# A block-attention and feed-forward kernel: token chunks of 512 against chunks of 512, 384 and 512

## The chip, the core and the metric

The kernel runs on one core of a Trainium2 chip. The metric is the device time of one execution in microseconds (us). Three runs of the kernel before took 1269.4, 1270.7 and 1272.47 us; the median is 1270.7 us.

## The reference: what is computed

Two stages follow each other. The first is attention over 8 batches, 8 heads, 576 positions and a head size of 64, masked by blocks of 64 positions. The second is a feed-forward network over the 4608 tokens that the attention gives.

```python
# _attn_ref: q, k, v of 8 x 8 x 576 x 64
scores = scale * np.matmul(q, k.transpose(0, 1, 3, 2))
mask = block_i >= block_j                      # blocks of 64
scores = np.where(mask, scores, -1000000000.0)
scores = scores - np.max(scores, axis=-1, keepdims=True)
attn = np.exp(scores)
attn = attn / (np.sum(attn, axis=-1, keepdims=True) + 1e-09)
return np.matmul(attn, v)
# _moe_ref: x of 4608 x 512, w_in 512 x 2048, w_out 2048 x 512
h = x @ w_in
g = np.where(h >= 1, h, np.where(h <= -1, 0.0, (h + 1) ** 2 / 4))
return g @ w_out
```

## The kernel before

**Attention.** Heads are worked on in pairs, four pairs a batch, 32 pairs in all. `attention_steps` is a generator that gives one step at a time, eight steps a pair, 258 in all. Within a step TensorE makes scores (`product`, two matmuls a tile, L482 and L485), transposes of the softmax that an earlier step left (`transposed`, L552), products of the softmax with v (`weighted`, L591) and transposes of q and k (L401, L442). VectorE (DVE) and ScalarE (ACT) do the softmax: maximum (L505), exponential (L509), sum, reciprocal, scaling (L515). Each of these TensorE results lies in a PSUM bank that `work_bank` hands out, and the bank is free for its next user once DVE and ACT have read it. `store_x` (or `both`, for the first two batches) writes the result, split into a high and a low half, into the rings `xh` and `xl`, which hold 1536 tokens.

**Feed-forward.** The tokens go in nine chunks of 512 (`TCH`), and each chunk over 16 slices of the hidden size. One slice has two half-steps. `ffn_in` makes 12 matmuls of 512 columns into the one bank of `ph` (4 parts of 128 of the model size, times 3 products of high and low halves; L770), and then ACT, DVE and POOL make `gh` and `gl` of it (L779, L780, L783, L784, L785). `ffn_out` makes 12 matmuls of 512 columns (L794 and L799: four token tiles of 128, times 3 products) into four banks `po`, which hold the sums of the chunk over all 16 slices. `ffn_out` of a slice comes one half-step after `ffn_in` of the next one. Each slice loads 512 KB of `w_out` (`wo`, L787) from DRAM; two buffers hold them.

**PSUM.** The eight banks are: three `ps_w` for the attention, one `ps_h` for `ph`, four `ps_o` for the sums. Before the feed-forward starts, the attention takes banks of `ps_o` and `ps_w` by turns; after that it has the three of `ps_w`.

**Order.** The loop at the end of the kernel runs the attention's steps. From step `START` = 36 on it runs one feed-forward half-step after each attention step; what is left after step 257 runs by itself. There are 288 half-steps: 222 beside the attention and 66 after it. A scheduler then moves single instructions where data or banks come late; from about 300 us on, the order on TensorE is that of the code but for a few rows. Names: `qk` is the transposed input of q and k, `prr` a softmax tile after its way through a DMA copy, `x` (`x32`) the attention's output before it is split.

Of the kernel before, what the change touches and what calls it, by code (L numbers as in the profile page):

```python
# [8 lines left out]
F32 = mybir.dt.float32  # L9
F32R = mybir.dt.float32r  # L10
# [13 lines left out]
def block_attn_then_ffn(  # L24
# [9 lines left out]
    nc = tc.nc  # L34
    B, H, S, D = q.shape
    NT, DM = out.shape
    DF = w_in.shape[1]
    P = 128
# [4 lines left out]
    NPAIR = H // 2  # L43
    NCC = DM // P
    NFC = DF // P
    TCH = 512
    NCH = NT // TCH
    NTT = TCH // P
    RING = 3 * TCH
    G0 = 256  # L50
    G1 = S - G0
# [14 lines left out]
    att1 = ctx.enter_context(tc.tile_pool(name="att1", bufs=1))  # L66
# [3 lines left out]
    ffn = ctx.enter_context(tc.tile_pool(name="ffn", bufs=2))  # L70
# [2 lines left out]
    dram = ctx.enter_context(tc.tile_pool(name="dram", bufs=1, space=bass.MemoryType.DRAM))  # L73
    ps_w = ctx.enter_context(tc.tile_pool(name="ps_w", bufs=3, space=bass.MemoryType.PSUM))
    ps_h = ctx.enter_context(tc.tile_pool(name="ps_h", bufs=1, space=bass.MemoryType.PSUM))
    ps_o = ctx.enter_context(tc.tile_pool(name="ps_o", bufs=NTT, space=bass.MemoryType.PSUM))

    banks = {"free": True, "n": 0}

    def work_bank(name):  # L80

        banks["n"] += 1
        if banks["free"] and banks["n"] % 2:
            return ps_o.tile([P, 512], F32, tag="po", name=name)
        return ps_w.tile([P, 512], F32, tag="work", name=name)


# [140 lines left out]
    spare = {"n": 0, "of": []}  # L228

    def as_float32r(src, plain):  # L230

        if plain:
            if not spare["of"]:
                spare["of"] = [t_[:, :NTL, :, :].rearrange("p t h d -> p (t h d)") for t_ in vsr]
                spare["of"].append(att1.tile([P, S], F32R, tag="x32", name="prs")[:, :TCH])
# [3 lines left out]
            if src.shape[1] > TCH:  # L239
                moved.append(spare["end"])  # L240
            for i, dst in enumerate(moved):
                n = min(TCH, src.shape[1] - i * TCH)
                nc.sync.dma_start(dst[:, :n].bitcast(F32), src[:, i * TCH : i * TCH + n])
            return moved
        moved = []
        for c0 in range(0, src.shape[1], TCH):
            n = min(TCH, src.shape[1] - c0)
            pool, tag = ((conv, "bits"), (conv2, "work"))[c0 > 0]
            dst = pool.tile([P, TCH], F32R, tag=tag, name="prr")
            nc.sync.dma_start(dst[:, :n].bitcast(F32), src[:, c0 : c0 + n])  # L250
            moved.append(dst)
        return moved


    class Pair:
# [141 lines left out]
        def turned_raw(self, j):  # L397

            ps = work_bank("ps_qk")
            for t in range(NTL):  # L400
                nc.tensor.transpose(  # L401
                    ps[:, t * P : (t + 1) * P].bitcast(F32R), self.qk[:, j * NTL + t, :, :], ident_r
                )
            self.parted(
                lambda x: x[:, j, :SM].rearrange("p (c t) -> p c t", t=NTL),
                ps[:, :SM].rearrange("p (t c) -> p c t", t=NTL),
            )
            for a, bt, hi0 in ((qa, qb, 0), (ka, kb, D)):
# [138 lines left out]
                nc.vector.tensor_tensor(out=lo, in0=ps, in1=hi.bitcast(F32), op=ALU.subtract)  # L547

        def transposed(self, out, parts, c0, n):
            src = parts[c0 // TCH][:, c0 % TCH : c0 % TCH + n] if self.hop else parts[0][:, c0 : c0 + n]  # L550
# [210 lines left out]


    def ffn_in(c, fc):
        at = (c * TCH) % RING
        ph = ps_h.tile([P, 512], F32, tag="ph", name="ph")
        fs = slice(fc * P, (fc + 1) * P)
        xs = slice(at, at + TCH)
        for cc in range(NCC):
            for i, (w, x) in enumerate(((wih, xh), (wih, xl), (wil, xh))):
                nc.tensor.matmul(  # L770
                    ph, w[:, cc, fs], x[:, cc, xs],
                    start=(cc == 0 and i == 0), stop=(cc == NCC - 1 and i == 2),
                )


        t_ = ffn.tile([P, TCH], F32, tag="t", name="t")
        gh = ffn.tile([P, TCH], F32R, tag="gh", name="gh")
        gl = ffn.tile([P, TCH], F32R, tag="gl", name="gl")
# [5 lines left out]
        nc.scalar.copy(gh, t_)  # L784
        nc.gpsimd.tensor_tensor(out=gl, in0=t_, in1=gh.bitcast(F32), op=ALU.subtract)  # L785
        wo = ffn.tile([P, 2, DM], F32R, tag="wo", name="wo")
        nc.sync.dma_start(wo.bitcast(F32), wo_split[fc])  # L787
        return gh, gl, wo

    def ffn_out(po, c, fc, gh, gl, wo):  # L790
        for tt in range(NTT):
            ts_ = slice(tt * P, (tt + 1) * P)
            for w in range(2):
                nc.tensor.matmul(  # L794
                    po[tt], gh[:, ts_], wo[:, w, :], start=(fc == 0 and w == 0), stop=False
                )
        for tt in range(NTT):
# [4 lines left out]
        for tt in range(NTT):  # L802
# [7 lines left out]
            r0 = c * TCH + tt * P  # L810
            nc.sync.dma_start(out[r0 : r0 + P, :], ob)

    def feed_forward():
        prev = None
        for c in range(NCH):
            for fc in range(NFC):
                cur = (c, fc, *ffn_in(c, fc))
                yield
                if prev is not None:
                    if prev[1] == 0:  # L820
                        po = [ps_o.tile([P, DM], F32, tag="po", name="po") for _ in range(NTT)]
                    ffn_out(po, *prev)
                    yield
                prev = cur
        ffn_out(po, *prev)
        yield
# [10 lines left out]
    converted = 0  # L837
    for i, _ in enumerate(attention_steps()):
        if i < START:
            want = (i + 1) * EARLY // START  # L840
        else:
            want = max(
                EARLY + (i - START + 1) * (NFC // GROUP * PART - EARLY) // (2 * NFC - 4 * GROUP),
                ((i - START) // (2 * GROUP) + 1) * PART,
            )
# [39 lines left out]
```

## Time and profile before

| what | value |
|---|---|
| median of three runs | 1270.7 us (1269.4 to 1272.47) |
| profiled execution, its own time | 1269.69 us |
| its span, first to last instruction | 1267.9 us |
| TensorE matmul busy | 1200.1 us, 95% |
| VectorE busy | 887.0 us, 70% |
| ScalarE busy | 703.2 us, 55% |
| GpSimd busy | 394.6 us, 31% |
| mean granted TensorE clock | 0.981 |

The busy time of TensorE counts a matmul from its start to the modelled end of its way through the array, so that neighbours overlap: what a matmul costs is the distance from its start to the next one's start. The share over the whole span mixes four stages: the attention alone (to about 155 us), the attention of the first batches beside the first chunk (to about 286 us), the attention beside the other chunks (to about 1080 us), and the last chunks alone.

### The profile page before, as it was taken

How to read it: one execution, taken by the hardware profiler on the slowest of the kernel's cores; microseconds unless marked ns; L12 is line 12 of the kernel's file. 1: busy time of each engine (PE TensorE's matmuls, PEld its weight loads, DVE VectorE, ACT ScalarE, POOL GpSimd, SP SyncE). 2: the span in 40 equal slices, each digit the busy share in tenths (PEclk: the TensorE clock that was granted, in tenths of full speed). 3: DMA queues.
4: the chain of work that ended last, by engine and by line, in shares of the span. 5: the costliest groups of instructions: out<-in, count | busy, mean ns of one | idle time of the engine just before them, and what ended most of it. 6: DMA issues, size and time to landing. Idle time of an engine off the chain costs nothing.

```text
span 1267.9 us, 20253 instructions
## 1 busy us (share of the span) xinstructions
PE 1200.1 (95%) x6280; PEld 998.8 (79%) x6280; DVE 887.0 (70%) x2188; ACT 703.2 (55%) x1827; POOL 394.6 (31%) x430
## 2 busy tenths in 40 slices
PE   5888889899999999999999999999999999999998
PEld 4666667678888888888888888888888888888886
DVE  8898877758777777777777777787777777322222
ACT  5787656646566655665656655566556555222222
POOL 3555655522222222222222222222222222222222
PEclk9888988999999999999999999999999999999999
DMA  5566666667888655555554655465556433422432
GB/s 158 167 176 215 203 228 197 217 198 237 260 273 266 215 162 158 154 175 163 156 162 145 187 157 152 138 189 153 160 154 190 137 128 118 132 87 98 133 100 100
DMA packets 185259, 215.43 MB, mean 170 GB/s; under 512 B 113840, under 2 KB 132272, under 8 KB 184384
## 3 DMA queue, kind: packets, MB, share of 16 engines
q1 hardware_dynamic: 185152, 214.14, 54.9%
q8 instruction: 50, 0.82, 0.3%
q14 instruction: 57, 0.47, 0.1%
HBM read 134.74 MB, written 31.98 MB: 131 GB/s over the span
## 4 chain that ended last, share of the span: by engine, by line
PE 69%; DVE 16%; ACT 6%; issue 5%; DMA 1%; POOL 1%; SPq 1%; ACTq 0%; POOLq 0%; DVEq 0%
PE ph L770 29%; PE po L794 15%; PE po L799 7%; PE ps_av L591 7%; PE ps_s L482 4%; ACT pr L509 3%; PE ps_s L485 3%; DVE t L780 2%; PE ps_t L552 2%; DVE t L783 2%; ACT t L779 2%; DVE pb L547 2%; DVE nm L505 2%; DVE sm L491 1%; DVE pr L515 1%
## 5 line engine op out<-in xcount | busy, mean ns | idle before, releaser
L785 POOL TENSOR_TENSOR gl<-t,gh 128x512 fp32r<-128x512 f32 x144 | 187.5, 1302 | 510.2 <-ACT gh L784 333.2
L794 PE MATMUL po<-wo,gh 128*128 128x512 f32 x1152 | 296.1, 397 | 0.5 <-DMA wo<-wo_split 0.3
L794 PEld LDWEIGHTS po<-wo,gh 128*128 128x128 f32 x1152 | 212.5, 189 | 44.5 <-DMA wo<-wo_split 0.7
L770 PE MATMUL ph<-xh,wih 128*128 128x512 f32 x576 | 232.9, 404 | 1.6 <-DVE t L783 1.6
L770 PE MATMUL ph<-xh,wil 128*128 128x512 f32 x576 | 228.8, 397 | 0.0
L770 PE MATMUL ph<-xl,wih 128*128 128x512 f32 x576 | 227.8, 396 | 0.5 <-DVE xl L627 0.5
L780 DVE SCALAR_TENSOR_TENSOR t<-t 128x512 f32<-128x512 f32 x144 | 101.5, 705 | 168.0 <-ACT t L779 165.2
L779 ACT ACTIVATE t<-ph 128x512 f32<-128x512 f32 x144 | 85.9, 597 | 173.8 <-PE ph L770 173.8
L509 ACT ACTIVATE pr<-ps_s,nm 128x128 f32<-128x128 f32 (+3 forms) x256 | 134.1, 527 | 60.5 <-DVE nm L505 58.4
L784 ACT CAST gh<-t 128x512 fp32r<-128x512 f32 x144 | 89.5, 621 | 120.3 <-DVE t L783 120.0
L799 PE MATMUL po<-wo,gl 128*128 128x512 f32 x576 | 155.6, 392 | 0.0
L482 PE MATMUL ps_s<-ka,qa 68*128 68x288 f32 (+4 forms) x384 | 135.3, 367 | 15.0 <-ACT pr L509 5.4
L379 POOL TENSOR_TENSOR vsr<-vn,vsr 128x256 fp32r<-128x256 f32 (+1 forms) x96 | 55.2, 576 | 246.2 <-ACT vsr L378 244.6
L770 PEld LDWEIGHTS ph<-xh,wil 128*128 128x128 f32 x576 | 109.5, 190 | 23.8
L770 PEld LDWEIGHTS ph<-xh,wih 128*128 128x128 f32 x576 | 109.8, 191 | 21.7 <-DVE t L783 2.3
L799 PEld LDWEIGHTS po<-wo,gl 128*128 128x128 f32 x576 | 108.7, 189 | 23.1
L505 DVE TENSOR_REDUCE nm<-ps_s 128x1 f32<-128x128 f32 (+3 forms) x256 | 118.8, 482 | 10.4 <-PE ps_s L485 9.4
L770 PEld LDWEIGHTS ph<-xl,wih 128*128 128x128 f32 x576 | 109.7, 190 | 20.5 <-DVE xl L627 0.9
L485 PE MATMUL ps_s<-kb,qb 128*128 128x288 f32 (+4 forms) x384 | 121.1, 322 | 0.0
L515 DVE TENSOR_SCALAR pr<-pr,sm 128x128 f32<-128x128 f32 (+3 forms) x256 | 107.3, 440 | 5.4
L783 DVE TENSOR_TENSOR t<-ph,t 128x512 f32<-128x512 f32 x144 | 98.7, 686 | 2.2
L491 DVE TENSOR_SCALAR sm<-sm 128x1 f32<-128x1 f32 (+1 forms) x224 | 52.0, 232 | 68.3 <-ACT pr L509 65.7
(111 smaller groups left out, 1871.4 us busy)
## 6 DMA issues: line engine op xcount, KB each, us to landing
wo<-wo_split SPq DMA_DIRECT2D x144, 512.0 KB, 3.5
prr<-pr SPq DMA_DIRECT2D x96, 192.0 KB, 2.5
prr<-pr SPq DMA_DIRECT2D x72, 256.0 KB, 2.8
out_dram<-ob SPq DMA_DIRECT2D x36, 256.0 KB, 2.9
bits<-in_moe_w_in_dram SPq DMA_DIRECT2D x32, 256.0 KB, 3.5
bits<-in_moe_w_out_dram SPq DMA_DIRECT2D x32, 256.0 KB, 3.0
wo_split<-ws SPq DMA_DIRECT2D x16, 512.0 KB, 2.9
qa<-qb SPq DMA_DIRECT2D x63, 128.0 KB, 2.4
```

Of the source, the lines that this page charges most:

```text
L482: nc.tensor.matmul(ps, qa[:KA, j, c0 : c0 + P], ka[:KA, j, k0 : k0 + n], start=first, stop=False)
L485: nc.tensor.matmul(ps, qb[:, j, c0 : c0 + P], kb[:, j, k0 : k0 + n], start=False, stop=last)
L505: nc.vector.tensor_reduce(out=nm[:, i : i + 1], in_=ps[:, cs], axis=AX.X, op=ALU.max, negate=True)
L509: nc.scalar.activation(pr[:, cs], ps[:, cs], AF.Exp, bias=nm[:, i : i + 1], scale=1.0, accum_out=sm[:, i : i + 1],)
L515: nc.vector.tensor_scalar_mul(pr[:, cs], pr[:, cs], sm[:, i : i + 1])
L770: nc.tensor.matmul(ph, w[:, cc, fs], x[:, cc, xs], start=(cc == 0 and i == 0), stop=(cc == NCC - 1 and i == 2),)
L779: nc.scalar.activation(t_, ph, AF.Relu, bias=0.5, scale=0.5)
L780: nc.vector.scalar_tensor_tensor(out=t_, in0=t_, scalar=1.0, in1=t_, op0=ALU.min, op1=ALU.mult)
L783: nc.vector.tensor_tensor(out=t_, in0=ph, in1=t_, op=ALU.max)
L785: nc.gpsimd.tensor_tensor(out=gl, in0=t_, in1=gh.bitcast(F32), op=ALU.subtract)
L794: nc.tensor.matmul(po[tt], gh[:, ts_], wo[:, w, :], start=(fc == 0 and w == 0), stop=False)
L799: nc.tensor.matmul(po[tt], gl[:, ts_], wo[:, 0, :], start=False, stop=fc == NFC - 1)
```

## The change

The chunks of tokens become: one of 512, eight of 384, two of 512, eleven in all. A chunk of 384 has three token tiles, so its sums need three banks. `ps_o` has three banks now, and the eighth bank (`ps_x`) serves the sums of the 512 chunks and, while chunks of 384 run, the attention: there it takes turns "wwwx", four banks in all. Before the feed-forward starts the turns are "woxwowo", seven banks.

The chunks of 384 do not divide the ring of 1536 tokens at the offset of 512: the chunks that start at tokens 1280 and 2816 lie over its end, at places 1280 to 1535 and 0 to 127. Each of their matmuls in `ffn_in` becomes two, of 256 and of 128 columns, with the same weights.

The pace is given by a table. `BEGIN` is the attention step at which each chunk starts: 36, 68, 99, 119, 139, 163, 183, 203, 227; the last two chunks would start at 259 and 279, past the attention's end at 257. The 32 half-steps of a chunk are spread over the steps to the next entry: 31 to 32 steps (chunks 0, 1 and 8), 20 steps (2, 3, 5, 6) or 24 (4, 7). Of 352 half-steps, 287 are run by step 257 and 65 after it.

```diff
+    NARROW = 384
+    CHUNKS = [(0, TCH)] + [(TCH + i * NARROW, NARROW) for i in range(MID)]
+    CHUNKS += [(t0, TCH) for t0 in range(CHUNKS[-1][0] + NARROW, NT, TCH)]
+    NTT = NARROW // P
...
+    ps_x = ctx.enter_context(tc.tile_pool(name="ps_x", bufs=1, space=bass.MemoryType.PSUM))
     ps_o = ctx.enter_context(tc.tile_pool(name="ps_o", bufs=NTT, space=bass.MemoryType.PSUM))
-    banks = {"free": True, "n": 0}
+    banks = {"turns": "woxwowo", "n": 0}
     def work_bank(name):
+        turns = banks["turns"]
+        turn = turns[banks["n"] % len(turns)]
         banks["n"] += 1
-        if banks["free"] and banks["n"] % 2:
+        if turn == "o":
             return ps_o.tile([P, 512], F32, tag="po", name=name)
+        if turn == "x":
+            return ps_x.tile([P, 512], F32, tag="px", name=name)
         return ps_w.tile([P, 512], F32, tag="work", name=name)
...
     def ffn_in(c, fc):
-        at = (c * TCH) % RING
+        t0, n = CHUNKS[c]
+        at = t0 % RING
+        runs = [(0, at, min(n, RING - at))]
+        if at + n > RING:
+            runs.append((RING - at, 0, at + n - RING))
         for cc in range(NCC):
             for i, (w, x) in enumerate(((wih, xh), (wih, xl), (wil, xh))):
-                nc.tensor.matmul(
-                    ph, w[:, cc, fs], x[:, cc, xs],
-                    start=(cc == 0 and i == 0), stop=(cc == NCC - 1 and i == 2),
-                )
+                for c0, x0, m in runs:
+                    nc.tensor.matmul(
+                        ph[:, c0 : c0 + m], w[:, cc, fs], x[:, cc, x0 : x0 + m],
+                        start=(cc == 0 and i == 0 and c0 == 0),
+                        stop=(cc == NCC - 1 and i == 2 and c0 + m == n),
+                    )
...
     def ffn_out(po, c, fc, gh, gl, wo):
-        for tt in range(NTT):
+        for tt in range(CHUNKS[c][1] // P):
...
                         po = [ps_o.tile([P, DM], F32, tag="po", name="po") for _ in range(NTT)]
+                        if CHUNKS[prev[0]][1] > NARROW:
+                            po.append(ps_x.tile([P, DM], F32, tag="px", name="po"))
...
+    BEGIN = [START]
+    for t0, n in CHUNKS[1:]:
+        ready = -(-(t0 + n) // S) * 8 * NPAIR + 3
+        BEGIN.append(max(ready, BEGIN[-1] + 20))
+    BEGIN[1] = START + 2 * NFC
...
+            c = sum(i >= x for x in BEGIN) - 1
+            left = BEGIN[c + 1] - BEGIN[c] if c + 1 < len(BEGIN) else 2 * NFC
+            due = 2 * NFC * c + min(2 * NFC, (i - BEGIN[c] + 1) * 2 * NFC // left)
...
-            banks["free"] = False
-            next(ffn_steps, None)
+            banks["turns"] = "www" if i < BEGIN[1] + 2 else "wwwx"
+            for _ in range(due - done):
+                next(ffn_steps, None)
+            done = due
```

The first place is on TensorE, in the second step of a pair of heads: the last transposes of q and k (`turned_last`, L442 before, L452 now), with the transposes and scores ahead of it and the feed-forward half-step behind it. The brackets name whose progress a row waits for. Before:

```order
L799 MATMUL po<-wo,gl 128x512 x3
L552 MATMUL ps_t<-ident_r,prr 128x128 [waits DMAHW0_49,DVE_49]
L552 MATMUL ps_t<-ident_r,prr 128x128 x3
L482 MATMUL ps_s<-ka,qa 128x384 [waits Activation_49]
L485 MATMUL ps_s<-kb,qb 128x384
L442 MATMUL ps_qk<-ident_r,qk 128x128 [waits DVE_49,PE_49]
L770 MATMUL ph<-xh,wih 128x512
```

Now, beside a chunk that has 20 steps:

```order
L785 MATMUL ph<-xh,wil 128x384
L562 MATMUL ps_t<-ident_r,prr 128x128 [waits DMAHW3_49,PE_49]
L562 MATMUL ps_t<-ident_r,prr 128x128 x3
L492 MATMUL ps_s<-ka,qa 128x384 [waits PE_49]
L495 MATMUL ps_s<-kb,qb 128x384
L452 MATMUL ps_qk<-ident_r,qk 128x128 [waits Activation_49]
L810 MATMUL po<-wo,gh 128x512 [waits DMAHW5_49]
```

The transpose waited for DVE, which read the bank of three users before; now it waits for ACT, which reads the bank of four users before, and the half-step behind it is another one.

The second place is on TensorE too, in the chunk that starts at token 1280: the matmuls of `ffn_in`. Before, and below it now:

```order
L770 MATMUL ph<-xh,wih 128x512
L770 MATMUL ph<-xl,wih 128x512
L770 MATMUL ph<-xh,wil 128x512
L770 MATMUL ph<-xh,wih 128x512
L770 MATMUL ph<-xl,wih 128x512
```

```order
L815 MATMUL po<-wo,gl 128x512 x2
L785 MATMUL ph<-xh,wih 128x256 [waits DVE_49]
L785 MATMUL ph<-xh,wih 128x128
L785 MATMUL ph<-xl,wih 128x256
L785 MATMUL ph<-xl,wih 128x128
L785 MATMUL ph<-xh,wil 128x256
L785 MATMUL ph<-xh,wil 128x128
```

Each matmul of 384 columns stands there as one of 256 and one of 128, each with a weight load of its own, 24 in the half-step in place of 12; in the other narrow chunks it is one row of 128x384.

More of the change, by code (lines that the diff above doesn't have):

```diff
@@ L46, in block_attn_then_ffn @@
     TCH = 512
-    NCH = NT // TCH
-    NTT = TCH // P
+    NARROW = 384
+    BANK = 512
+    MID = (NT - 3 * TCH) // NARROW
+    CHUNKS = [(0, TCH)] + [(TCH + i * NARROW, NARROW) for i in range(MID)]
+    CHUNKS += [(t0, TCH) for t0 in range(CHUNKS[-1][0] + NARROW, NT, TCH)]
+    NTT = NARROW // P
     RING = 3 * TCH
@@ L234, in as_float32r @@
                 spare["of"] = [t_[:, :NTL, :, :].rearrange("p t h d -> p (t h d)") for t_ in vsr]
-                spare["of"].append(att1.tile([P, S], F32R, tag="x32", name="prs")[:, :TCH])
+                spare["of"].append(att1.tile([P, S], F32R, tag="x32", name="prs")[:, :BANK])
                 spare["end"] = att1.tile([P, G0 + P], F32R, tag="pa11", name="pre")[:, :BLK]
@@ L238, in as_float32r @@
             spare["n"] += 1
-            if src.shape[1] > TCH:
+            if src.shape[1] > BANK:
                 moved.append(spare["end"])
             for i, dst in enumerate(moved):
-                n = min(TCH, src.shape[1] - i * TCH)
-                nc.sync.dma_start(dst[:, :n].bitcast(F32), src[:, i * TCH : i * TCH + n])
+                n = min(BANK, src.shape[1] - i * BANK)
+                nc.sync.dma_start(dst[:, :n].bitcast(F32), src[:, i * BANK : i * BANK + n])
             return moved
         moved = []
-        for c0 in range(0, src.shape[1], TCH):
-            n = min(TCH, src.shape[1] - c0)
+        for c0 in range(0, src.shape[1], BANK):
+            n = min(BANK, src.shape[1] - c0)
             pool, tag = ((conv, "bits"), (conv2, "work"))[c0 > 0]
-            dst = pool.tile([P, TCH], F32R, tag=tag, name="prr")
+            dst = pool.tile([P, BANK], F32R, tag=tag, name="prr")
             nc.sync.dma_start(dst[:, :n].bitcast(F32), src[:, c0 : c0 + n])
@@ L549, in transposed @@
         def transposed(self, out, parts, c0, n):
-            src = parts[c0 // TCH][:, c0 % TCH : c0 % TCH + n] if self.hop else parts[0][:, c0 : c0 + n]
+            src = parts[c0 // BANK][:, c0 % BANK : c0 % BANK + n] if self.hop else parts[0][:, c0 : c0 + n]
             if self.hop:
@@ L763, in ffn_in @@
     def ffn_in(c, fc):
-        at = (c * TCH) % RING
-        ph = ps_h.tile([P, 512], F32, tag="ph", name="ph")
+        t0, n = CHUNKS[c]
+        at = t0 % RING
+        ph = ps_h.tile([P, TCH], F32, tag="ph", name="ph")[:, :n]
         fs = slice(fc * P, (fc + 1) * P)
-        xs = slice(at, at + TCH)
+        runs = [(0, at, min(n, RING - at))]
+        if at + n > RING:
+            runs.append((RING - at, 0, at + n - RING))
         for cc in range(NCC):
             for i, (w, x) in enumerate(((wih, xh), (wih, xl), (wil, xh))):
-                nc.tensor.matmul(
-                    ph, w[:, cc, fs], x[:, cc, xs],
-                    start=(cc == 0 and i == 0), stop=(cc == NCC - 1 and i == 2),
-                )
-        t_ = ffn.tile([P, TCH], F32, tag="t", name="t")
-        gh = ffn.tile([P, TCH], F32R, tag="gh", name="gh")
-        gl = ffn.tile([P, TCH], F32R, tag="gl", name="gl")
+                for c0, x0, m in runs:
[4 more added lines that the diff above has]
+                    )
+        t_ = ffn.tile([P, TCH], F32, tag="t", name="t")[:, :n]
+        gh = ffn.tile([P, TCH], F32R, tag="gh", name="gh")[:, :n]
+        gl = ffn.tile([P, TCH], F32R, tag="gl", name="gl")[:, :n]
         nc.scalar.activation(t_, ph, AF.Relu, bias=0.5, scale=0.5)
@@ L796, in ffn_out @@
                 )
-        for tt in range(NTT):
+        for tt in range(CHUNKS[c][1] // P):
             ts_ = slice(tt * P, (tt + 1) * P)
@@ L801, in ffn_out @@
             return
-        for tt in range(NTT):
+        for tt in range(CHUNKS[c][1] // P):
             ob = conv.tile([P, DM], F32, tag="bits", name="ob") if tt % 2 else conv2.tile(
@@ L809, in ffn_out @@
                 nc.vector.tensor_copy(ob, po[tt])
-            r0 = c * TCH + tt * P
+            r0 = CHUNKS[c][0] + tt * P
             nc.sync.dma_start(out[r0 : r0 + P, :], ob)
@@ L814, in feed_forward @@
         prev = None
-        for c in range(NCH):
+        for c in range(len(CHUNKS)):
             for fc in range(NFC):
@@ L836, in block_attn_then_ffn @@
     ffn_steps = feed_forward()
-    converted = 0
+    BEGIN = [START]
[3 more added lines that the diff above has]
+    BEGIN[1] = START + 2 * NFC
+    converted = done = 0
     for i, _ in enumerate(attention_steps()):
@@ L841, in block_attn_then_ffn @@
         else:
+            c = sum(i >= x for x in BEGIN) - 1
+            left = BEGIN[c + 1] - BEGIN[c] if c + 1 < len(BEGIN) else 2 * NFC
+            due = 2 * NFC * c + min(2 * NFC, (i - BEGIN[c] + 1) * 2 * NFC // left)
             want = max(
-                EARLY + (i - START + 1) * (NFC // GROUP * PART - EARLY) // (2 * NFC - 4 * GROUP),
-                ((i - START) // (2 * GROUP) + 1) * PART,
+                EARLY + due * (NFC // GROUP * PART - EARLY) // (2 * NFC - 4 * GROUP),
+                ((due - 1) // (2 * GROUP) + 1) * PART,
             )
```

## The prediction

> **What bounds the kernel.** I read the page's engine table and slices first, then busy time by stage, then single matmuls.
>
> ```profile
> PE 1200.1 (95%) x6280; PEld 998.8 (79%) x6280; DVE 887.0 (70%) x2188; ACT 703.2 (55%) x1827; POOL 394.6 (31%) x430
> PE   5888889899999999999999999999999999999998
> DVE  8898877758777777777777777787777777322222
> PEclk9888988999999999999999999999999999999999
> ```
>
> ```profile
> 0.00:155.00 155.00, 121.89 (x629) 98.26 (x630) 134.84 (x394) 109.91 (x326) 78.98 (x103) 0.93 0.61 185
> 155.00:286.00 131.00, 115.49 (x523) 88.82 (x522) 91.54 (x224) 74.29 (x207) 61.20 (x74) 0.91 0.66 208
> 286.00:1080.00 794.00, 779.88 (x4327) 661.13 (x4326) 610.76 (x1500) 474.71 (x1223) 210.46 (x219) 1.00 0.58 175
> 1080.00:1268.00 188.00, 182.79 (x807) 150.64 (x805) 49.89 (x73) 44.27 (x74) 43.99 (x34) 0.99 0.33 108
> ```
>
> The columns are the stretch, its length, then busy us of PE, PEld, DVE, ACT and POOL, the granted clock, the DMA share and GB/s. Three limits show. To 155 us DVE is busy 134.84 of 155 (87%) and PE waits for it. From 286 to 1080 us PE is busy 779.88 of 794: 14.1 us of idle time in the whole stage in which the change acts. After 1080 us PE runs alone. So in the stage that matters a matmul added is time added, and a wait removed can give back only what PE loses now.
>
> How fast PE can go is in the starts of its matmuls and weight loads:
>
> ```profile
> 704.87 0.39 PE L770 MATMUL ph<-xh,wil 128*128 128x512 f32 x1
> ...
> 706.91 0.39 PE L770 MATMUL ph<-xh,wil 128*128 128x512 f32 x1
> ```
>
> ```profile
> 702.62 1.31 PE L591 MATMUL ps_av<-pb,vsr 128*128 128x320 f32 x8
> 703.77 0.33 PE L591 MATMUL ps_av<-pcs,vsr 128*128 128x64 f32 x2
> ...
> 707.88 1.03 PE L591 MATMUL ps_av<-pa,vsr 128*128 128x256 f32 x8
> 708.75 2.03 PE L794 MATMUL po<-wo,gh 128*128 128x512 f32 x8
> ```
>
> ```profile
> 707.77 1.00 PEld L591 LDWEIGHTS ps_av<-pa,vsr 128*128 128x128 f32 x8
> 708.69 0.77 PEld L794 LDWEIGHTS po<-wo,gh 128*128 128x128 f32 x4
> ```
>
> Between the first two rows lie nine distances: (706.91 - 704.87)/9 = 0.227 us for 512 columns. The group at 707.88 has, by the code, four matmuls of 256 and four of 128 columns in pairs, a mean of 192; they take (708.75 - 707.88)/8 = 0.109 us each, and their weight loads (708.69 - 707.77)/8 = 0.115 us each. By columns, 192 would take 0.085 us. So short matmuls go at the pace of their weight loads, 0.109 to 0.115 us.
>
> **The waits that a fourth bank can touch.**
>
> ```profile
> PE ps_qk L442 <- DVE x L614: 8.9, 23, 0.4
> PE ps_s L482 <- ACT pr L509: 5.2, 17, 0.3
> ```
>
> ```profile
> 711.30 0.20 ACT L509 ACTIVATION_READ_ACCUMULATOR pr<-ps_s,nm 128x1 f32 x1
> 711.53 0.36 ACT L613 COPY xtmp<-ps_av 64x256 f32<-64x256 f32 x1
> 712.08 0.34 PE L485 MATMUL ps_s<-kb,qb 128*128 128x384 f32 x1
> 712.25 0.43 DVE L614 TENSOR_TENSOR x<-ps_av,xtmp 64x256 f32<-64x256 f32 x1
> 712.83 0.25 PE L442 MATMUL ps_qk<-ident_r,qk 128*128 128x128 f32 x1 [0.41 <-DVE x L614]
> ```
>
> These two waits add up to PE's 14.1 us (286 to 1080 us). L442 needs the bank that L614 reads, three users back. The loss is more than the 0.41 us shown, since a matmul's modelled end counts as busy: L442 starts 0.75 us after L485, where 384 columns need some 0.18, so 0.57 us x 23 = 13.1 us.
>
> **The change, part by part.** Half-steps outside chunks 1 to 8 are as before (chunks 0, 9, 10 are 512 wide).
>
> (a) Narrow matmuls in the six unsplit chunks: 6 x 16 x 12 = 1152 of 384 columns. By columns alone one costs 0.75 x 0.227 = 0.170 us. The group at 702.62 (six of 320 and two of 192, 2304 columns in 703.77 - 702.62 = 1.15 us) and the 512 rows give two equations for a price a column and a price a matmul: 0.37 ns and 0.037 us, so 0.179 for 384, too high since its short ones go at the loads' pace. I take 0.173: 1152 x 0.003 = +3.5 us (0 to +10). The matmuls of `ffn_out` are the same in number and width: 0.
>
> (b) The two chunks over the ring's end: 2 x 16 x 12 = 384 matmuls become 256 + 128. Mean 192 columns, two loads: the L591 group's case. A pair costs 2 x 0.109 = 0.218 us against 0.170: 384 x 0.048 = +18 us (+23 at the loads' 0.115; 0 if the second load hid). That both halves use the same weights saves nothing where loads are issued per matmul, and they are: `ffn_out` uses each `gh` block twice in a row, and has as many loads as matmuls:
>
> ```profile
> L794 PE MATMUL po<-wo,gh 128*128 128x512 f32 x1152 | 296.1, 397 | 0.5 <-DMA wo<-wo_split 0.3
> L794 PEld LDWEIGHTS po<-wo,gh 128*128 128x128 f32 x1152 | 212.5, 189 | 44.5 <-DMA wo<-wo_split 0.7 <-ACT gh L784 0.6
> ```
>
> The Trainium skill ("TensorE: Matmul & The Clock Gate", section "Back-to-back issue gap") prices an isolated warm matmul at N/2.4 + 2.5 ns, which would make a pair of 256 and 128 dearer than one of 384 by 2.5 ns, 1 us in all. Its section "LDWEIGHTS (loading the stationary operand)" gives a load of 128 columns 128/1.2 = 107 ns, by which a pair cannot be under 214 ns, some 17 us in all; the 0.109 us of the L591 group agrees with the second.
>
> (c) Four banks for the attention in chunks 1 to 8. L442 then waits for the bank of four users back, the scores of the step before, which ACT left at 711.30 + 0.20 = 711.50 in the rows above, before PE ended L485. That wait goes, and most of L482's, which is for an exponential three users back. At most 13.1 + 5.2 = -18 us; I take -15, since each half-step that covers these chains gets shorter (12 x 0.173 = 2.08 us for `ffn_in` and 9 x 0.227 = 2.04 for `ffn_out` against 2.72). The other end is nothing gained, or 5 us lost, if DVE and ACT run that much later against PE. Next late is the score bank of (c) itself, with 0.7 us to spare.
>
> (d) The pace. Chunks 1 and 8 give 61 attention steps only one narrow half-step each.
>
> ```profile
> L442 PE MATMUL ps_qk<-ident_r,qk x24: 221/252/254, 274.4 to 1047.2; 128*128 128x128 f32 x24
> ```
>
> ```profile
> 300.00:1000.00 700.00, 686.92 (x3816) 582.40 (x3814) 541.67 (x1331) 421.45 (x1087) 187.67 (x197) 1.00 0.60 181
> ```
>
> ```profile
> 300.00:1000.00 700.00, 57.34 (x83) 1.00 0.60 181
> ```
>
> ```profile
> 300.00:1000.00 700.00, 56.80 (x83) 1.00 0.60 181
> ```
>
> ```profile
> L547 DVE TENSOR_TENSOR pa<-ps_t,pa 128x384 fp32r<-128x384 f32 x48 | 26.6, 555 | 21.3 <-ACT pa L545 21.3
> ```
>
> L442 comes once a pair: (1047.2 - 274.4)/23/8 = 4.20 us a step, of which 2.72 is the half-step and 0.1 the waits, so 1.38 is the attention's own PE time. A sparse step needs 1.38 + 2.06 = 3.44 us of PE. DVE works 541.67/700 x 4.20 = 3.25 us a step; its two feed-forward operations (the two short rows, L780 and L783) take (57.34 + 56.80)/83/2 = 0.69 of it. With some 0.56 at 384 columns (L547's 555 ns; two, half of each a step) it needs 3.12, 91% of 3.44. The highest share that DVE holds in any stage is the 87% ahead of 155 us; at that, a step is 3.59 us, and 61 steps lose 9 us; if DVE keeps up, nothing. I take +4. The dense chunks (20 steps) need 1.38 + 1.6 x 2.06 = 4.68 us of PE and 2.56 + 0.8 x 1.12 = 3.46 of DVE (74%): 0.
>
> (e) The rest. 32 more loads of `wo`:
>
> ```profile
> wo<-wo_split SPq DMA_DIRECT2D x144, 512.0 KB, 3.5
> ```
>
> A load is issued when its buffer's last reader is done and is needed two half-steps and at least one attention step later, 2.04 + 2.08 + 1.38 = 5.5 us against 3.5; the rows of L794 show 0.5 us waited before. On SP only copies of later softmax tiles stand behind it, which need three steps. If that cover went, each late load would hold up PE directly. ACT, DVE and POOL each get 32 more rounds of three to five short operations, beside PE: 0. Chunks 2, 5 and 8 read tokens stored in the same step, behind an `ffn_out` and the first nine matmuls (2.04 + 1.56 us) that cover the split; 0 to 3 us, taken as 0. Ahead of step 36 seven banks turn evenly in place of four and three; DVE bounds that stage, so 0, but the scheduler's other order there may move it 4 us either way.
>
> The sum, against the profiled execution's own 1269.7 us: +3.5 + 18 - 15 + 4 = +10.5, so 1280.2. The median of the runs lies 1.0 above that execution: 1281.
>
> **Rivals.** A, faster: the second load of the same weights hides, and (b) is 0. Then 1281 - 18 = 1263. It decides at a pair price of 0.190 us, where (b) is 8 us and the sum is no change. For it speaks that the pair's 0.170 us of streaming leaves the array free for one load of 0.115; against it that two loads don't fit, and that no row has loads closer. 12 in 100. B, no change: the banks give the full 18 us, the stage before 155 us gains 4 from its seven banks, DVE keeps up in (d): 1281 - 3 - 4 - 4 = 1270. For it speaks PE's idle there, 155 - 121.9 us; against it DVE's 87%. 10 in 100. C, much slower: DVE holds PE in the sparse chunks (9 to 12 us), the pairs cost the loads' 0.115 (+5), the banks give 10: 1281 + 6 + 5 + 5 = 1297. 18 in 100. D: the wait at L442 is replaced by one for the scores' bank, (c) gives nothing, all else as forecast: 1296; within C's share.
>
> **The numbers.** My forecast, 1273 to 1291, has 60 in 100. Faster or slower than no change is told from 0.2%, 2.5 us here, which is about what this measurement can tell. Faster: A and a small part of B, 0.14. Within 0.2%: most of B, 0.09. Slower: 0.77. The range leaves out most of A and the upper half of C: 1267 to 1296.
>
> **What the trace after would show.** (a) Starts of `ph` matmuls 0.172 to 0.175 us apart in the narrow chunks. (b) Half-steps of 24 matmuls over some 2.6 us, their weight loads 0.108 or more apart, against 2.08 unsplit; 2.04 would be rival A. (c) No wait of the L442 line on L614. (d) A step of 3.45 to 3.6 us in chunks 1 and 8, DVE near 90% there. (e) PE waiting for `wo` below 1 us. I am wrong if equal weights are loaded once, or if a wait that the profile before does not show, for `ph`'s one bank or for x at a chunk's start, takes over.

## The result, and the profile after

The changed kernel takes 1311.31 us (median of four runs, 1309.44 to 1316.84), the kernel before 1270.5 us in the same comparison: 41 us more, 1.032 by these two medians. The ratio on record is 1.035, 95% interval 1.0329 to 1.0372. It does not follow from these medians, but fits the 1267 us that the kernel before took in every later comparison; by it the change costs 44 us. Either way that is about four times the 10.5 us of the forecast. The profiled execution took 1311.25 us, its span is 1308.6 us. The engine table, three rows of slices and the busy time by stage of the changed kernel:

```profile
PE 1227.4 (94%) x7048; PEld 1074.1 (82%) x7048; DVE 907.7 (69%) x2256; ACT 707.1 (54%) x1887; POOL 401.6 (31%) x462
PE   5878897999999999999999999999999999999998
DVE  8987877758887776677877777677776888322222
PEclk9898889899999999999999999999999999999999
```

```profile
0.00:155.00 155.00, 119.13 (x605) 95.28 (x606) 131.03 (x390) 108.31 (x321) 80.80 (x105) 0.91 0.60 181
155.00:289.00 134.00, 116.33 (x558) 92.62 (x557) 94.00 (x229) 76.72 (x213) 60.76 (x74) 0.94 0.68 211
289.00:1120.00 831.00, 809.86 (x5086) 736.77 (x5085) 632.30 (x1565) 477.84 (x1281) 216.26 (x250) 1.00 0.61 188
1120.00:1308.00 188.00, 182.10 (x804) 149.44 (x802) 50.40 (x75) 44.21 (x74) 43.74 (x34) 1.00 0.31 105
```

The mean granted clock is the same (0.981 in both), the first stages are as long as before within 3 us, the last as well; the loss lies beside the narrow chunks. There TensorE's matmuls are busy longer, and its idle time is 831 - 809.86 = 21.1 us where it was 14.1.

Both parts can be measured from the starts of the matmuls. First the prices, from TensorE's timeline of the changed kernel: a half-step in chunk 1 (unsplit), and one in the chunk over the ring's end, where a row merges the two pieces of a pair.

```profile
347.57 0.34 PE L785 MATMUL ph<-xl,wih 128*128 128x384 f32 x1
...
348.96 0.33 PE L785 MATMUL ph<-xh,wih 128*128 128x384 f32 x1
```

```profile
519.98 0.40 PE L785 MATMUL ph<-xh,wih 128*128 128x256 f32 x2
...
521.83 0.39 PE L785 MATMUL ph<-xh,wil 128*128 128x256 f32 x2
```

Eight distances each: (348.96 - 347.57)/8 = 0.174 us for 384 columns, (521.83 - 519.98)/8 = 0.231 us for a pair of 256 and 128. Against 0.170, three quarters of 512 columns, this is 1152 x 0.0037 = 4.3 us and 384 x 0.0608 = 23.3 us, 27.6 us together.

Second, what is left. I give each matmul the median distance to its successor that its shape has in the kernel before (for the new shapes 0.174, 0.171 and 0.060 us) and add up by attention step how far the starts deviate. The sums of four other kernels, told below, stand beside:

| deviation from streaming prices, us | before | after | e2: three banks | e14: one a step | e9: after, no clamp | e12: before, no clamp |
|---|---|---|---|---|---|---|
| to step 68 | 76.2 | 77.3 | 79.3 | 80.6 | 73.2 | 67.6 |
| 68 to 99, chunk 1 (31 steps) | 4.9 | 8.4 | 11.3 | 6.7 | 3.4 | 1.1 |
| 99 to 227, chunks 2 to 7 | 19.7 | 17.8 | 26.0 | 31.9 | 5.2 | 3.2 |
| from 227, chunk 8 and the end | 5.0 | 14.7 | 23.2 | 14.8 | 5.0 | 1.1 |
| sum | 105.8 | 118.2 | 139.8 | 134.0 | 86.8 | 73.0 |

So 27.6 us are prices and 118.2 - 105.8 = 12.4 us are waits; the two make 40.0 of the 40.7 us between the spans. The wait at the last transposes (L442 before, L452 now) is gone but for three short ones, as its row shows, and others stand in the list of TensorE's waits from 286 to 1120 us:

```profile
L452 PE MATMUL ps_qk<-ident_r,qk x24: 218/223/281, 276.3 to 1093.2; 128*128 128x128 f32 x24
...
  ACT pr L519: 0.9, 3
```

```profile
PE ps_qk L411 <- ACT pr L545: 5.5, 7, 1.7
PE ph L785 <- DVE t L799: 5.1, 7, 1.6
PE ph L785 <- POOL xl L667: 2.7, 3, 1.2
PE ps_t L562 <- DMA prr<-pr: 1.8, 2, 1.2
PE ps_s L492 <- DVE sm L501: 1.4, 2, 0.8
PE ps_t L562 <- DVE t L796: 1.3, 1, 1.3
```

The first is the bank of `scores_last`, four users back: a bank of scores, but at L411 and not at the transposes that (c) was about. The second is the one bank of `ph`; the third is a chunk that reads tokens stored in the same step, which (e) took as 0. The forecast gave the second and third kind as a sign that it is wrong, and the list of the kernel before has neither.

The same sums can be cut at the start of each chunk. In the changed kernel the deviation per attention step is then 0.27 us in chunk 1 and 0.45 from chunk 8 on (one half-step a step), 0.25 and 0.19 in chunks 4 and 7 (1.33), and 0.15, 0.03, 0.14 and 0.06 in chunks 2, 3, 5 and 6 (1.6). In the kernel before, with one wider half-step a step, it is 0.12 to 0.16 throughout. So the less feed-forward work stands behind an attention step, the more is lost there.

### The profile page after: what moved, and what is told of

Same layout as the page of the kernel before. It is cut to its first block, busy times and chain, and to the rows that moved or that the text cites. A ratio compares the mean times of both kernels' runs of the same rounds, so it can differ in the third digit from the quotient of the medians.

```text
span 1308.6 us, 22001 instructions
## 1 busy us (share of the span) xinstructions
PE 1227.4 (94%) x7048; PEld 1074.1 (82%) x7048; DVE 907.7 (69%) x2256; ACT 707.1 (54%) x1887; POOL 401.6 (31%) x462
## 5 line engine op out<-in xcount | busy, mean ns | idle before, releaser
L801 POOL TENSOR_TENSOR gl<-t,gh 128x384 fp32r<-128x384 f32 (+1 forms) x176 | 193.4, 1099 | 622.5 <-ACT gh L800 358.6
L785 PE MATMUL ph<-xh,wih 128*128 128x384 f32 (+2 forms) x832 | 260.4, 338 | 7.0 <-DVE t L799 6.8
L785 PE MATMUL ph<-xl,wih 128*128 128x384 f32 (+2 forms) x832 | 257.3, 334 | 3.3 <-POOL xl L667 3.3
L785 PE MATMUL ph<-xh,wil 128*128 128x384 f32 (+2 forms) x832 | 256.7, 334 | 0.0
L796 DVE SCALAR_TENSOR_TENSOR t<-t 128x384 f32<-128x384 f32 (+1 forms) x176 | 114.8, 652 | 192.1 <-ACT t L795 190.0
L795 ACT ACTIVATE t<-ph 128x384 f32<-128x384 f32 (+1 forms) x176 | 91.5, 520 | 187.2 <-PE ph L785 185.7
L800 ACT CAST gh<-t 128x384 fp32r<-128x384 f32 (+1 forms) x176 | 95.1, 540 | 145.7 <-DVE t L799 145.1
L785 PEld LDWEIGHTS ph<-xh,wih 128*128 128x128 f32 x832 | 149.3, 190 | 23.2 <-DVE t L799 10.1
L799 DVE TENSOR_TENSOR t<-ph,t 128x384 f32<-128x384 f32 (+1 forms) x176 | 103.4, 588 | 3.2 <-PE ps_av L601 0.5
L492 PEld LDWEIGHTS ps_s<-ka,qa 68*128 68x128 f32 x384 | 74.7, 195 | 16.7 <-ACT kb L437 6.3
```

The costliest lines, as they stand in the source:

```text
L492: nc.tensor.matmul(ps, qa[:KA, j, c0 : c0 + P], ka[:KA, j, k0 : k0 + n], start=first, stop=False)
L785: nc.tensor.matmul(ph[:, c0 : c0 + m], w[:, cc, fs], x[:, cc, x0 : x0 + m], start=(cc == 0 and i == 0 and c0 == 0), stop=(cc == NCC - 1 an ...
L796: nc.vector.scalar_tensor_tensor(out=t_, in0=t_, scalar=1.0, in1=t_, op0=ALU.min, op1=ALU.mult)
```

## The experiments

Ratios are to the kernel before, run on the same chip; there its median was 1267 us, so 1% is 12.7 us. Savings and losses against the changed kernel are taken from its 1.035, 1311.31 us against some 1267.

**e1: no pairs.**

```diff
-        at = t0 % RING
+        at = min(t0 % RING, RING - n)
```

> The changed kernel, with the two chunks that lie over the ring's end reading one stretch of 384 tokens (the last of the ring) in place of 256 + 128; so they read the wrong tokens, and 384 matmuls of ph are not split. Theory of the weight loads: the changed kernel's pairs stand 171 + 60 = 231 ns apart against 174 unsplit, so 384 x 0.057 = 22 us go: 1311 becomes 1289, ratio to the kernel before 1.015. Rival, the order and the waits make the whole loss and the pairs hide in them: under 5 us go, ratio above 1.030.

Measured: 1289.43 us, ratio 1.0179 (1.016 to 1.0197), so 1.71% or 21.7 us less than the changed kernel. The deviations stayed (119.1 us). The pairs' price stands, and rival A falls.

**e2: three banks for the attention.**

```diff
-            banks["turns"] = "www" if i < BEGIN[1] + 2 else "wwwx"
+            banks["turns"] = "www"
```

> The changed kernel with the attention on three banks all the time (turns www beside narrow chunks); the eighth bank idles there. If the fourth bank removed the wait at the last transposes of q and k and gave nothing back, taking it away costs the 12.6 us that this wait cost before, 1311 becomes 1324 (ratio 1.042). If the new waits (27 us, at the ph bank, at L411 and at the chunks' starts) have taken its place whatever the banks, the time stays at 1311 within 4 us (1.035).

Measured: 1326.33 us, ratio 1.0471 (1.0445 to 1.0497): 15 us more (its profiled execution lies 5.6 us above the median, so its deviations in the table are some 5 us too large for that). The fourth bank is worth what step (c) said. But what came back is only for a small part the wait at the last transposes (L442 before, L452 here, 2.0 us); the rest are waits that the kernel before did not have or had shorter, so the size came out right for other reasons than the forecast gave:

```profile
PE ps_s L492 <- ACT pr L545: 9.2, 8, 1.9
PE ps_av L601 <- DVE kb L405: 6.0, 10, 1.4
PE ph L785 <- DVE t L799: 4.4, 7, 1.4
PE ps_t L562 <- DMA prr<-pr: 2.2, 2, 1.8
PE ps_qk L452 <- DVE x L624: 2.0, 6, 0.3
```

With three banks in both, the new pace and width add 139.8 - 105.8 = 34 us of deviation, of which the bank takes 15 to 20 off. That is the term that the forecast had at 4.

**e3, e5, e6: GpSimd's subtraction.** In the changed kernel VectorE stands still in places. Its timeline (TensorE, VectorE, ScalarE and GpSimd, rows left out) beside chunk 8:

```profile
1043.01 0.28 PE L495 MATMUL ps_s<-kb,qb 128*128 128x256 f32 x1
1043.28 0.99 POOL L801 TENSOR_TENSOR gl<-t,gh 128x384 fp32r<-128x384 f32 x1 [2.16 <-ACT gh L800]
1043.36 0.93 DVE L543 TENSOR_TENSOR nm<-nm 128x1 f32<-128x1 f32 x1
1044.33 0.50 ACT L545 ACTIVATE pr<-ps_s,nm 128x288 f32<-128x288 f32 x1 [1.18 <-DVE nm L543]
...
1044.97 0.50 PE L411 MATMUL ps_qk<-ident_r,qk 128*128 128x128 f32 x2 [1.68 <-ACT pr L545]
```

L543 works on 128x1 elements and takes 0.16 us where nothing of GpSimd overlaps it; here it ends when GpSimd's gl ends. Summed over VectorE after 286 us, operations that overlap GpSimd last 34 us longer than their shapes need, some 24 of them under gl and 9 under the split of x (L667); in the kernel before it is 13.6 us. e3 has `nc.scalar.copy(gl, t_)` in place of the subtraction, e5 (changed) and e6 (before) have

```diff
-        nc.gpsimd.tensor_tensor(out=gl, in0=t_, in1=gh.bitcast(F32), op=ALU.subtract)
+        gl = gh
```

> The changed kernel with gl made by a copy on ScalarE of t in place of GpSimd's subtraction (the low half is left out, its values are wrong, the matmuls are the same). Theory of the collisions: VectorE operations that meet GpSimd's gl stand still till it ends, 34 us in all after 286 us in the changed kernel against 14 before, and they sit on the chains that TensorE waits for; then the stretched time falls under 3 us, the waits over 150 ns from 27 to about 14 us, and the time by some 12 us to 1299 (ratio 1.022). Rival, the thinner cover of the new pace alone: GpSimd doesn't matter, ScalarE has 0.47 us a slice more, and the time stays or grows, 1311 to 1320.

> The changed kernel without GpSimd's subtraction gl; the third product of the sums uses gh again (the low half is left out), so no engine takes over the work and the matmuls are the same in number and size. Theory of the collisions: the waits over 150 ns after 276 us fall from 27.5 to about 15 us, and the stage before 276 us gains 12 as in the run with gl on ScalarE: 1311 becomes 1286 (ratio 1.015). Rival, the cover and the pace: the waits after 276 us stay above 23 us, and only the early stage gains: 1299 (1.025).

> The kernel before without gl, as in e5 (the low half is left out). The early stage gains 12 us by the run with gl on ScalarE. Theory of the collisions: in the kernel before, gl holds up the sum's reciprocal (L491, 0.49 us in place of 0.15) that stands ahead of L614 on VectorE, and TensorE's wait at L442 falls from 0.55 to about 0.2 us a pair, 8 us more: 1251 (0.985). Rival: the wait at L442 stays, 1258 (0.990).

Measured: e3 1296.64 us, ratio 1.0232 (1.0212 to 1.0252); e5 1290.41 us, 1.0179 (1.0159 to 1.0199); e6 1246.01 us, 0.9834 (0.9813 to 0.9856). e3's 15 us came from the stage ahead of step 68 (deviation 65.1 in place of 77.3); behind it the waits over 150 ns stayed (28.8 us, 30.1 in the changed kernel, counted from the first transposed pair at 257 us). e5, which has no copy on ScalarE in its place, took these to 20.2 us, and e6 those of the kernel before from 16.6 to 9.0. The collisions are real and dear, yet in both kernels: e5 against e6 is 3.5% again. They don't explain the loss.

**e4: chunk 8 one step later** (`BEGIN[8] += 1`).

> The changed kernel with the last narrow chunk one attention step later (BEGIN[8] 228), which turns round which half-step follows which attention step there, at nearly the same pace. If the waits of that chunk (11 us from 1000 to 1130 us) come from where the half-steps fall, those at L411 (1.8 us each) and the wait for xl at the chunk's start go: 5 to 8 us less, 1305. If they come from the thin cover of the sparse pace, nothing changes within 2 us.

Measured: 1303.49 us, ratio 1.028 (1.0263 to 1.0298), 9 us less. From step 227 on the deviation went from 14.7 to 9.0 us. At nearly the same pace, where the half-steps fall decides over some of the waits.

**e7: another order of the chunks, no pairs.**

```diff
-    CHUNKS = [(0, TCH)] + [(TCH + i * NARROW, NARROW) for i in range(MID)]
-    CHUNKS += [(t0, TCH) for t0 in range(CHUNKS[-1][0] + NARROW, NT, TCH)]
+    CHUNKS = [(i * NARROW, NARROW) for i in range(MID)]
+    CHUNKS += [(t0, TCH) for t0 in range(MID * NARROW, NT, TCH)]
...
-            banks["turns"] = "www" if i < BEGIN[1] + 2 else "wwwx"
+            banks["turns"] = "www" if i >= BEGIN[8] + 2 else "wwwx"
```

> The changed kernel with its chunks in another order: eight of 384 first, then three of 512, the pace by the same rule. No chunk lies over the ring's end, so the 384 pairs go (-22 us by the run with one range). The sparse chunks are then the first (beside batch 1) and one of 512 beside the last batch, which has the three banks and the pace of the kernel before. If the sparse narrow chunks make 17 us of the 27.5 us of waits, these fall to about 14 and the time is near 1280 (ratio 1.010); if any narrow chunk brings them, 1289 (1.017). Faster than the kernel before by no theory.

Measured: 1298.61 us, ratio 1.0246 (1.0227 to 1.0266), a miss for both expectations, by 1.5% and 0.8%. The pairs went, but the stage ahead of step 68 deviates by 87.8 us in place of 77.3, and the waits over 150 ns behind 257 us are still 25.2 us.

**e8: the kernel before, its last transposes later.**

```diff
                 cur.scores(0, 1)
-                cur.turned_last()
+                if not cur.far:
+                    cur.turned_last()
...
             yield
+            if cur and cur.far:
+                cur.turned_last()
             if far:
                 old.attn_v(1)
```

> The kernel before with one edit: from the third batch on, the last transposes of q and k (turned_last) are made at the start of a pair's third step in place of the end of its second, so that they ask for a bank one half-step later. If the wait at L442 (0.55 us x 23 = 12.6 us) is only the bank's lateness, it goes and nothing takes its place: 1258 (ratio 0.990). Rival: the next user of a bank (the products with v or the next transposes) waits instead: 1270 within 3 us (1.000).

Measured: 1278.03 us, ratio 1.0074 (1.005 to 1.0098): slower. L442's wait went and a larger one took its place, at the next users of the three banks, as the list of TensorE's waits (286 to 1080 us) shows:

```profile
PE ps_s L482 <- ACT pr L509: 16.5, 39, 0.6
```

**e9 and e12: less work for VectorE.** L796 (changed) or L780 (before), the clamp and square of each slice, is left out:

```diff
-        nc.vector.scalar_tensor_tensor(
-            out=t_, in0=t_, scalar=1.0, in1=t_, op0=ALU.min, op1=ALU.mult
-        )
```

> The changed kernel without VectorE's L796 (the clamp and square of the activation is left out), so that VectorE has 0.55 us less per slice and the ph bank comes free that much earlier. Theory that VectorE, 82 to 90% full beside the sparse chunks, is what TensorE waits for there: the deviation from streaming prices in the two sparse chunks (8.4 us in steps 68 to 98, 14.7 us from step 227 on) falls to under half, the waits for the ph bank (5.4 us) go, and with the early stage 20 us or more go: 1311 to 1290 (ratio 1.018). Rival, the place of the half-steps alone: only the ph waits and some of the early stage go, 1302 (1.027), and the sparse chunks keep 17 us or more.

> The kernel before without L780 (the clamp and square left out), the control of e9. There the changed kernel came to 1277 us with 11 us of waits after the early stage. If VectorE's fullness explains the waits that the change added, both kernels lose nearly all of them, and the gap is what matmuls and loads cost, 27.6 us (22 to 33): this one near 1250 (ratio 0.986). Rival: the kernel before gains as much as the changed one, 34 us, and the gap stays 41: 1236 (0.975).

Measured: e9 1277.3 us, ratio 1.0077 (1.0055 to 1.01); e12 1236.84 us, ratio 0.9753 (0.9736 to 0.977). The deviation in the sparse chunks fell from 8.4 + 14.7 to 3.4 + 5.0 us: most of TensorE's waits there hung on a late VectorE. But the kernel before gains nearly as much, and the gap between the two is still 41 us (it was 41 by the first medians, 44 by the ratio of 1.035): the rival of e12. So a late VectorE explains the waits, but not by itself the difference between the two kernels. The gap has the same two parts as before: about 28 us of prices and 86.8 - 73.0 = 13.8 us of deviation. In the kernel before nearly nothing is left to wait for (first list, 286 to 1080 us); in the changed one the reads of tokens just stored and a bank remain (second list, 286 to 1110 us):

```profile
PE ps_s L482 <- ACT pr L509: 0.4, 1, 0.4
```

```profile
PE ph L785 <- POOL xl L667: 2.3, 3, 1.1
PE ps_s L492 <- DVE pb L557: 1.8, 5, 0.4
PE ph L785 <- DMA qk<-rawk: 0.6, 1, 0.6
```

**e10 and e11: the addition of 1e-9 left out**, in the kernel before, and in the changed one with chunk 8 a step later.

```diff
-            nc.vector.tensor_scalar_add(total, total, EPS)
```

> The kernel before without the addition of 1e-9 to the softmax sums (L491); the sums hold exp(0) = 1, so in fp32 the addition changes no bit. The collisions of the kernel before sit on this instruction (13.3 us of standing still behind GpSimd's gl) and it is 52 us of VectorE's time. If TensorE's wait at L442 hangs on it as the run without gl suggests (12.6 to 5.1 us), 7 us go there and some in the early stage, where VectorE is 87% full: 1255 (ratio 0.989). Rival: the collisions move to the next instruction (the reciprocal or the scaling), and only the instruction's own time counts: 1266 (0.997).

> The changed kernel without the addition of 1e-9, and with its last narrow chunk one step later: the best of the changed kernel that the runs point to. Chunk 8 later gave 8 us, the addition gives some 10 in the early stage and the sparse chunks: 1293 (ratio 1.020). It stays slower than the kernel before, since 27.6 us are prices of matmuls and loads; if it came under 1280 these would not be fixed.

Measured: e10 1267.24 us, ratio 1.0001 (0.9986 to 1.0015), no change: the collisions moved to the scaling (7.2 us of standing still there), and L442 waited longer. e11 1297.68 us, ratio 1.0239 (1.0222 to 1.0256), the best of the changed kernel here with its own order and all its work but this addition, and still 30 us behind. No version that computes the whole came in below the kernel before.

**e13 and e14: the pace alone.** e13 is even from step 99 on, e14 has one half-step a step throughout.

```diff
+            if i >= BEGIN[2]:
+                due = 4 * NFC + (i - BEGIN[2] + 1) * 223 // 159
```

```diff
+            due = i - START + 1
```

> The changed kernel with an even pace from step 99 on: 223 half-steps over 159 attention steps (1.40 a step) in place of 20, 24 and 32 steps a chunk. Later chunks then read tokens of the ring that are already written over (wrong values; the work is the same), and chunks 5 and 8 no longer begin in the step that stores their tokens. If the unevenness of the pace (the sparse last chunk and the chunks' starts) makes the added waits, the deviation from streaming prices from step 99 on falls from 32 to about 18 us: 1297 (ratio 1.023). Rival, any narrow half-steps beside the attention bring them: 1311 within 4 us (1.035).

> The changed kernel with the pace of the kernel before, one half-step after each attention step, so that 130 half-steps are left for the end; the ring is written over before some chunks have read it (wrong values; the work is the same). Every step has then the thin cover of 2.06 us of the sparse chunk 1, but the half-steps fall as in the kernel before. If thin cover makes the waits, each step deviates from streaming prices by the 0.27 us of chunk 1: 190 x 0.27 = 51 us in place of 44, and the time is 1315 or more (ratio 1.038). If where the half-steps fall makes them, the deviation is that of the kernel before without its L442 wait, some 20 us, and the time is 1290 (1.018).

Measured: e13 1305.27 us, ratio 1.0308 (1.0291 to 1.0325), half-way between its two expectations: the end from step 227 fell from 14.7 to 5.6 us of deviation, but chunks 2 to 7, which had 1.33 or 1.6 half-steps a step and have 1.40, rose from 17.8 to 24.2. e14 1324.89 us, ratio 1.0449 (1.0422 to 1.0476): thin cover in every step, and the deviation from step 68 on is 53.4 us, where the place theory had 20. Its waits between 286 and 980 us, and its busy time from 600 to 900 us (PE, PEld, DVE, ACT, POOL):

```profile
PE ph L785 <- POOL xl L667: 8.6, 10, 1.2
PE ps_t L562 <- DMA prr<-pr: 7.0, 10, 1.7
PE ps_s L492 <- DVE sm L501: 4.2, 9, 0.8
```

```profile
600.00:900.00 300.00, 288.00 (x1792) 256.92 (x1792) 243.93 (x640) 192.30 (x521) 79.28 (x96) 0.99 0.61 182
```

Part of the wait for xl (11 us by the starts) may belong to the ring being written over while a chunk reads it; without all of it 42 us would be left, still twice what the place theory had.

## Why the prediction was wrong, point by point

The direction was right; the size was not. By the forecast's own terms:

- **(a)** was +3.5, and is 4.3 us.
- **(b)** was +18, and is 23.3 us by the starts, 21.7 by e1. The mechanism is the forecast's; the price is the loads' 0.115 us, which it had beside the 0.109 and left for the range's end. In the group of eight from which 0.109 came, the last short matmul's delay falls on the matmul behind the group, so the loads' own distance was the one to take: in the trace the first L794 behind the group stands 0.284 us from the next one, in place of 0.227. The Trainium skill ("TensorE: Matmul & The Clock Gate", section "LDWEIGHTS (loading the stationary operand)") gives a load's time as its columns / 1.2 ns, so 107 ns as an estimate for 128 columns. The traces agree for the pairs, where no load follows another within 108 ns and the mean is 115; the loads of the transposes stand closer, 82 ns at the least.
- **(c)** was -15. e2 measures 15 us, and L442's wait is gone. That the two sizes agree is partly luck: the forecast added up the waits at L442 and L482 of the kernel before (18 us), while the bank, at the new pace, holds off mostly other waits (e2's list).
- **(d)** was +4, and is the step that failed. With three banks the new width and pace add some 28 us of waits (e2's 34, less the 5.6 us that its profiled execution was above its median), so that bank and pace together are +12.4, not -11. Of the 34 us, 24.6 lie in the stretches with sparse chunks, where the forecast had 4, and 6.3 beside chunks 2 to 7, where it had 0. The forecast priced a sparse step by one engine's mean share: a loss only where VectorE would be fuller than the 87% it holds ahead of 155 us. The busy time of the changed kernel beside chunk 1, chunk 3 and chunk 8 shows that this bound means little:

```profile
311.00:397.00 86.00, 83.44 (x509) 74.63 (x508) 70.89 (x189) 55.83 (x156) 23.77 (x30) 1.00 0.81 244
520.00:595.00 75.00, 75.00 (x547) 69.96 (x546) 50.16 (x121) 37.99 (x100) 17.32 (x19) 1.00 0.51 155
1008.00:1092.00 84.00, 77.72 (x469) 69.86 (x470) 68.83 (x170) 51.19 (x140) 19.91 (x24) 0.98 0.53 165
```

  VectorE is 82% busy in both sparse chunks, below 87% and not near the 90% of the forecast, and TensorE loses 2.6 of 86 and 6.3 of 84 us. Beside chunk 3, with the long pairs, VectorE is 67% busy and TensorE loses nothing. By the starts of L452 a step took 3.60 us in chunk 1 (311.0 to 397.4 us, 24 steps) and 3.83 in chunk 8 (1031.9 to 1093.2 us, 16 steps), where 3.45 to 3.6 were forecast. What TensorE mostly waits for is an answer that VectorE gives late: its queue holds a step's softmax and the slice's activation one behind the other, and a shorter half-step leaves less time for it. The deviation per step by pace and e14 show the thin cover, e9 shows VectorE's part in the waits, e4 that the place of the half-steps counts too. That VectorE is what makes the difference between the two kernels is not shown: from step 68 on the changed kernel deviates 11.3 us more, and without the clamp still 8.2 us more (e9 against e12).
- **(e)**: beside the narrow chunks the loads of `wo` stayed hidden. Ahead of them, in chunk 0, TensorE waited 4.4 us for two loads (at 251.6 and 264.5 us), where it was 0.3 before and below 1 us was forecast:

```profile
L810 PE MATMUL po<-wo,gh 128*128 128x512 f32 x1152 | 305.0, 401 | 4.9 <-DMA wo<-wo_split 4.4 <-DVE ob L825 0.3
```

  The chunks that read tokens stored in the same step, taken as 0 of 0 to 3 us, wait 2.7 us by the list and up to 1.4 us each by the starts. The deviation to step 68 grew by only 1 us.
- **The rivals.** A fell by e1. One argument against it was misread, though: the forecast says that no row has loads closer, yet those of the transposes (L552) do stand closer in the kernel before. Those of the pairs don't. C named the right place, the sparse chunks, and its 1297 falls short by 14 us: it had 9 to 12 us there and the banks at -10. B is ruled out by the result. D came in part: a wait for a bank of scores appeared (L411, 5.5 us), but the bank's gain stayed. The case that came, the forecast's gain of the bank and a loss by pace larger than it, was no rival.

What stays open: how the 12.4 us divide among thin cover, the place of the half-steps and the chunks' starts. The deviation per step falls as the pace gets denser, but e4, e13 and e14 each move part of it, and they don't add up independently.

## What to carry to other kernels

Choose chunk widths and starts so that no chunk lies over the ring's end: here a matmul cut in two paid a weight load for the second piece, and the piece of 128 columns cost its load (0.115 us), not its columns (0.057 us, a quarter of 0.227). When a half-step that covers another pipeline's latency gets shorter, price the cover by a stage with as little of it, not by the busy share of an engine: here TensorE lost time beside a VectorE that was 82% busy. And measure a wait that is removed against the order it will stand in; here the fourth bank gave its 15 us, against a loss of some 28 us that the same edit made.

## What the runs showed of the hardware that was not expected

GpSimd's work makes VectorE stand still. In the kernel before, the sum's addition over two columns has a mean of 435 ns, over one column 151; without gl (second fence, e6) the first falls to 180 and the second stays:

```profile
L491 DVE TENSOR_SCALAR sm<-sm 128x2 f32<-128x2 f32 x64 | 27.8, 435 | 25.6 <-ACT pr L509 25.6
L491 DVE TENSOR_SCALAR sm<-sm 128x1 f32<-128x1 f32 x160 | 24.2, 151 | 42.7 <-ACT pr L509 40.1
```

```profile
L491 DVE TENSOR_SCALAR sm<-sm 128x2 f32<-128x2 f32 x64 | 11.5, 180 | 26.7 <-ACT pr L509 26.6
L491 DVE TENSOR_SCALAR sm<-sm 128x1 f32<-128x1 f32 x160 | 24.2, 151 | 43.4 <-ACT pr L509 40.8
```

The Trainium skill ("SBUF — State Buffer", section "Who interferes with whom") says that a VectorE instruction in a two-port mode contends with GpSimd for a shared pair of ports, which the first to issue holds for its whole instruction; one with two SBUF inputs contends with a GpSimd instruction that reads SBUF. The traces agree, down to an operation with two inputs on one column (L543) that took 0.93 us in place of 0.16. Which operation is hit hangs on the order, so a change of pace moves the collisions (13.6 us in the kernel before, 34 in the changed one). Gl's whole price, collisions and all, is 21 us in the kernel before (e6) and 22 in the changed one (e5).
